# Pairs 4 to 11 of a chunked state-space scan in 64-token chunks on small TensorE tiles, ahead of a gated feed-forward layer

## The chip, the core and the metric

The kernel runs on one core of a Trainium2 chip. The metric is device time in microseconds of one execution; less is better. TensorE (PE in the profile) multiplies into eight PSUM banks, VectorE (DVE) and ScalarE (ACT) read them out, GpSimd (POOL) works on SBUF, and SyncE (SP) issues most of the DMAs.

## What is computed

Two steps. The first is a scan with a decaying state for 4 x 8 = 32 heads over 768 tokens each, head size 32 and state size 16; the second is a feed-forward layer on all 3072 tokens of 8 x 32 = 256 channels.

```python
for c in range(nc):                       # chunks; the result does not depend on their length
    cum = np.cumsum(la, axis=-1)          # la: log of the decay a, inside the chunk
    L = np.exp(cum[..., :, None] - cum[..., None, :]) * causal
    M = np.einsum('bhin,bhjn->bhij', Cc, Bc) * L
    y_intra = np.einsum('bhij,bhjd->bhid', M, xc)
    y_inter = np.einsum('bhin,bhnd->bhid', Cc, state) * np.exp(cum)[..., None]
    y[:, :, sl] = y_intra + y_inter
    Bx = np.einsum('bhjn,bhjd->bhjnd', Bc, xc) * np.exp(cum[:, :, -1:] - cum)[..., None, None]
    state = np.exp(np.sum(la, axis=-1))[..., None, None] * state + np.sum(Bx, axis=2)
# then, with x the scan's result per token:
out = (np.maximum(x @ w_gate, 0.0) * (x @ w_val)) @ w_out     # 256 -> 1536 -> 256
```

## The kernel before

The 3072 tokens are handled as 12 pairs of two 128-token chunks; three pairs make one of the four sequences. B and C are scaled beforehand with products of the decays (`scale`, line 293, on GpSimd for most pairs), so that the scan itself is left with plain matmuls: the state is a running sum, and only the causal mask stays. Four heads of 32 partitions each are laid side by side (q from 0 to 3), and two sets of four heads (t is 0 or 1) share a row of B and C in 16 of the 32 partitions each.

For a pair the steps are: `turn` transposes C and B on TensorE (line 310), ScalarE and VectorE copy them out as BT and CT. `G` (line 358) multiplies B and C of each head in four row positions of 32 rows, 128 columns wide, into four banks (g0 to g3). `gevac` (line 371) takes those 128x512 results out under the causal mask: two banks by ScalarE with GpSimd's affine_select behind it, two and a half by VectorE with a multiplication by a mask. `state` (line 407) adds a chunk's B times x in PSUM (`astep`, line 391, tile A_ps) and copies the sum out under a mask (`sevac`, line 401, tile Sm, VectorE). `inter` (line 428) multiplies the state by C into the pair's y bank, `Dm` (line 442) adds the masked G times x in four column positions of 32 columns, and `yevac` (line 456) copies y to yT in bf16, on ScalarE. Pairs 0 to 3 ("wide") hold two neighbouring tokens per partition and reach yT in two copies.

The feed-forward layer runs in six blocks of 512 tokens. In block b, pairs P = 2b+2 and Q = 2b+3 go through the scan while the layer works on pairs 2b and W = 2b+1, W being finished at the beginning of the block. `gvh` (line 484) computes gate and value for 256 tokens in one bank, `gv` (line 470) for 512 tokens in two; ScalarE applies the relu (tile r), VectorE multiplies (tile h). `fout` (line 499) is the output matmul of 128 tokens, twelve matmuls of 256 columns. A block is: a few `gvh` on the first 256 tokens, the end of W (`inter`, `Dm`, `yevac`), the same `gvh` on the second 256 tokens, eight `gv` (six in block 1) with `turn` and `state` between them, `inter` of P, then four `fout` with `G`, `state`, `Dm` of P and Q between them. Block 5 has no P and Q.

The order on every engine is the order in the program text: `in_order` fixes it at the end. The waits are set by the framework, from who writes and reads a tile. PSUM is laid out as five shared banks (`bank`, line 66: gate, value, o, G and others), one for transposes (tp), one for y, one for A_ps. SP issues each pair's six loads at the start of a block, two pairs ahead, and the output stores.

Of the kernel before, what the change touches and what calls it, by code (L numbers as in the profile page):

```python
# [29 lines left out]
def kernel(  # L30
# [23 lines left out]
    PPB = NC // 2  # L54
    NBLK = T // 512

    const = ctx.enter_context(tc.tile_pool(name="const", bufs=1))
# [8 lines left out]
    def bank(name="bank", shape=(128, 512), dtype=FP32):  # L66
        return mm.tile(list(shape), dtype, tag="shared", bufs=NSHARED, name=name)

    NWIDE = 4
    st = {}
# [89 lines left out]
    causal(masks[:, 1:2], 1, True)  # L162
    causal(masks[:, 0:1], 1, False)
    weights(0, 4)
    xb1 = att.tile([128, 2 * NH * D], BF16, tag="xb", name="xb")
    st[1]["x"] = [xb1[:, i * NH * D:(i + 1) * NH * D] for i in range(2)]
# [23 lines left out]
    def keep_warm(n, cols=512):  # L190
        w = mm.tile([128, 512], FP32, tag="y", name="w")
        for _ in range(n):
            nc.tensor.matmul(out=w[:, 0:cols], lhsT=warm[:, 0:128], rhs=warm[:, 0:cols],
                             start=True, stop=True)
# [47 lines left out]
    def new_bs(p):  # L242
        st[p]["bs"] = att.tile([128, 4, 128], BF16, tag="bs", name="bs")
        bs = st[p]["bs"]
        if p < NWIDE:
            st[p]["tin"] = [[bs[:, 2 * j + r] for r in range(2)] for j in range(2)]
        else:
            st[p]["tin"] = [[bs[:, 2 * i + j] for i in range(2)] for j in range(2)]
            st[p]["B"] = st[p]["tin"][0]
# [32 lines left out]
    def to_x(p, eng, f=None):  # L282
        xb = att.tile([128, 2 * NH * D], BF16, tag="xb", name="xb")
        xr = st[p]["xr"].rearrange("s i h d -> s (i h) d")
# [67 lines left out]
    def backevac(p, eng):  # L352
        s = st[p]
        bx = att.tile([128, 2, 128], BF16, tag="bx", name="bx")
        copy(eng, bx, s.pop("bt"))
# [35 lines left out]
    def astep(p, i):  # L391
# [3 lines left out]
        if not A_ps:  # L395
            A_ps.append(mm.tile([128, 2, 128], FP32, tag="Aps", name="A_ps"))
        nc.tensor.matmul(  # L397
# [13 lines left out]
    def y_bank(s, apart=False):  # L411
        if "y" not in s:
            if apart:
                y0 = mm.tile([128, 2, 128], FP32, tag="y", name="y")
                s["y"] = [y0, bank("y1", (128, 2, 128))]
            else:
                y = mm.tile([128, 2, 2, 128], FP32, tag="y", name="y")
                s["y"] = [y[:, 0], y[:, 1]]
                s["ya"] = y
# [36 lines left out]
    def yevac(p, *engs):  # L456
        s = st.pop(p)
        dst = yT[:, :, p * 256:(p + 1) * 256]
# [3 lines left out]
        for t in range(2):  # L462
            copy(engs[t % len(engs)],
                 dst[:, t].rearrange("q (i m r) -> q i r m", i=2, r=2),
                 s["y"][t].rearrange("q i (r m) -> q i r m", r=2))


# [58 lines left out]
    new_bs(0)  # L526
    d0 = mm.tile([128, 2, 8], FP32, tag="Aps", name="d0")
    dec_wide(d0, 0, True)
# [9 lines left out]
    bevac(0, nc.vector)  # L538
    d1 = mm.tile([128, 2, 8], FP32, tag="Aps", name="d1")
    dec_wide(d1, 1, True)  # L540
# [30 lines left out]
    bevac(1, nc.scalar)  # L571
    cevac(1, nc.vector)

    def late_decay():
# [46 lines left out]
    for b in range(NBLK):  # L621
        P, Q, W = 2 * b + 2, 2 * b + 3, 2 * b + 1
        more = P < NPAIR
        for n in (P + 2, P + 3):
            if b and n < NPAIR:
                load(n, nc.sync)

        def at(name, *fs):
            return more and f == fs[min(b, len(fs) - 1)]

        nh = 6 if b < 2 else 4
        for f in range(nh):
            if b == 0 and f < 4:
                continue
            gvh(b, f, 0)
            if b and f == (4 if b == 1 else 1):
                if b == 1:
                    state(W, 1)
                inter(W, 0)
                inter(W, 1)  # L640
                Dm(W)
                yevac(W, nc.scalar)
        for f in range(nh):
            gvh(b, f, 1)
            if b == 1 and f in (0, 3):
                scale(P if f == 0 else Q, nc.gpsimd)
        for f in range(nh, NF):
            gv(b, f)
            if b == 0 and f == 6:
                scale(P, nc.gpsimd)  # L650
                for n in (3, 4, 5):
                    held(n)
            if at("scale", 11, 99, 4):
                for n in (Q,) if b == 0 else (P, Q):
                    scale(n, nc.gpsimd)
            if at("turn P", 8, 6, 5):
                turn(P)
                tevac(P, nc.scalar, nc.vector)
            if b == 0 and f == 9:
                back(P)  # L660
                backevac(P, nc.vector)
            if at("state P0", 10, 8, 7):
                state(P, 0)
            if at("state P1", 11, 10, 9):
                state(P, 1)
            if at("turn Q", 99, 9, 8):
                turn(Q)
                tevac(Q, nc.scalar, nc.vector)
        if b == 0:
            decay()  # L670
        if more:
            inter(P, 0)
            inter(P, 1)
        fout(b, 0)
        foevac(b, 0)
        if more:
            G(P)
# [6 lines left out]
        if b == 0:  # L684
            back(Q)
            backevac(Q, nc.vector)
        if more and b > 0:
            state(Q, 0)
        if b == 0:
            for n in range(NB):  # L690
                nc.vector.reciprocal(fac[:, n, :, 0], fac[:, n, :, 1])
        fout(b, 2)
        foevac(b, 2)
        if more:
            Dm(P)
            yevac(P, nc.scalar)
            G(Q)
            gevac(Q)
            state(Q, 1 if b else 0)
        fout(b, 3)  # L700
# [33 lines left out]
```

## Time and profile before

| | us |
|---|---|
| median of three runs | 132.06 (131.21 to 132.6) |
| the profiled execution | 131.31, its span 129.5 |
| TensorE clock granted in it | 0.997 |
| block 1 in the chain, 35.41 to 54.31 | 18.90 |
| block 2, 54.31 to 72.82 | 18.51 |
| block 3, 72.82 to 91.34 | 18.52 |
| block 4, 91.34 to 109.74 | 18.40 |
| block 5, 109.74 to 126.14, no P and Q | 16.40 |

The groups of instructions that the change touches, from the page (line, engine, operation, out<-in, shapes, count, then busy us and mean ns of one, then idle time of the engine before them and what ended it):

```profile
L383 DVE TENSOR_TENSOR gs<-g,masks 128x512 bf16<-128x512 f32 x24 | 15.5, 686 | 12.8 <-PE g L364 6.4
L252 ACT CAST yT<-y 128x512 bf16<-128x512 f32 (+1 forms) x15 | 7.4, 522 | 10.5 <-PE y L449 8.2
L377 ACT CAST gs<-g 128x512 bf16<-128x512 f32 x12 | 7.1, 589 | 9.3 <-PE g L364 9.3
L405 DVE TENSOR_TENSOR Sm<-A_ps,smask 128x256 bf16<-128x256 f32 x20 | 8.3, 414 | 0.9 <-PE A_ps L397 0.9
L252 POOL CAST xb<-xr 128x512 bf16<-128x512 f32 x11 | 6.7, 613 | 2.3 <-DMA xr<-in_x_dram 1.6
```

Shown by form, the ScalarE cast to yT takes 449 ns at 128x256 and 585 at 128x512, VectorE's 446 at 128x256, the RECIPROCAL of 128x16 from PSUM (line 532) 252, and GpSimd's scaling multiplication of 128x256 (line 278) 621. Times in the chain of waits run from the end of one piece of work to the end of the next, so a piece's start there can be up to 0.2 us behind its start in the timeline. The idle column matters only for the engine that sets the end.

### The profile page before, as it was taken

The numbers are of one execution on the slowest core, as the hardware profiler recorded it, in microseconds if no ns is written. First come the engines' busy times: TensorE is split into PE (matmuls) and PEld (weight loads), VectorE is DVE, ScalarE is ACT, GpSimd is POOL, SyncE is SP. The second block draws the span as 40 slices with busy tenths as digits, with TensorE's granted clock in tenths as the row PEclk, the third lists the DMA queues.
The fourth block names the chain that finished last, engine by engine and source line by source line (L and its number), as shares of the span: only waits on it lengthen the run. The fifth ranks groups of instructions, "written<-read, shape, count | busy, mean of one in ns | idle before, by whom it ended". The sixth has DMA issues, their size and how long they took to land.

```text
span 129.5 us, 3159 instructions
## 1 busy us (share of the span) xinstructions
PE 121.3 (94%) x1144; PEld 82.2 (63%) x1151; DVE 93.4 (72%) x222; ACT 77.8 (60%) x171; POOL 42.4 (33%) x79
## 2 busy tenths in 40 slices
PE   6977889999999999999999999999999999999990
PEld 2534566468777467784567875477865577854770
DVE  4679958966987896578965878965799965587410
ACT  4063658735588754688644797745887645876410
POOL 7998591035292003390003760011930032000000
PEclk9999999999999999999999999999999999999998
DMA  3999999996999498269951198562200002200021
GB/s 65 148 178 170 177 149 178 191 143 67 118 127 202 47 126 113 86 116 113 96 86 48 41 142 119 53 95 81 83 3 0 0 5 81 81 0 0 5 103 59
DMA packets 71151, 11.97 MB, mean 92 GB/s; under 512 B 64864, under 2 KB 71072, under 8 KB 71136
## 3 DMA queue, kind: packets, MB, share of 16 engines
q1 hardware_dynamic: 63408, 8.49, 42.2%
q0 software_dynamic: 5360, 2.75, 16.5%
q10 hardware_dynamic: 2368, 0.52, 2.3%
q8 instruction: 9, 0.15, 0.5%
q14 instruction: 6, 0.05, 0.1%
HBM read 11.11 MB, written 3.15 MB: 110 GB/s over the span
## 4 chain that ended last, share of the span: by engine, by line
PE 84%; DMA 5%; DVE 5%; POOL 2%; issue 1%; SPq 1%; ACT 0%; DVEq 0%
PE o L504 25%; PE gv L492 18%; PE val L478 15%; PE gate L475 13%; DMA xr<-in_x_dram 5%; PE y L449 3%; PE g L364 3%; PE tp L310 2%; PE A_ps L397 2%; PE y L438 2%; DVE h L482 1%; DVE gs L383 1%; POOL gs L158 1%; DVE CT L332 1%; PE dall L233 1%
## 5 line engine op out<-in xcount | busy, mean ns | idle before, releaser
L504 PE MATMUL o<-wo,h 128*128 128x256 bf16 x288 | 34.7, 273 | 0.0
L482 DVE TENSOR_TENSOR h<-r,val 128x512 bf16<-128x512 bf16 x44 | 30.2, 686 | 5.1 <-ACT r L481 3.0
L481 ACT ACTIVATE r<-gate 128x512 bf16<-128x512 f32 x44 | 26.3, 597 | 9.9 <-PE gate L475 9.1
L158 POOL TENSOR_SCALAR_AFFINE_SELECT gs<-gs 128x512 bf16<-128x512 bf16 (+1 forms) x24 | 12.2, 529 | 57.0 <-ACT gs L377 57.0
L504 PEld LDWEIGHTS <-h 128*128 128x128 bf16 x288 | 27.4, 98 | 4.5 <-issue 1.3
L496 DVE TENSOR_TENSOR h<-r,gv 128x256 bf16<-128x256 bf16 x56 | 23.3, 421 | 6.6 <-ACT r L495 6.0
L478 PE MATMUL val<-yT,wv 128*128 128x512 bf16 x88 | 26.2, 379 | 0.3
L475 PE MATMUL gate<-yT,wg 128*128 128x512 bf16 x82 | 24.9, 379 | 0.0
L383 DVE TENSOR_TENSOR gs<-g,masks 128x512 bf16<-128x512 f32 x24 | 15.5, 686 | 12.8 <-PE g L364 6.4
L495 ACT ACTIVATE r<-gv 128x256 bf16<-128x256 f32 x56 | 21.5, 385 | 2.7 <-PE gv L492 0.6
L492 PE MATMUL gv<-yT,wg 128*128 128x256 bf16 x112 | 21.6, 273 | 0.1
L492 PE MATMUL gv<-yT,wv 128*128 128x256 bf16 x112 | 21.4, 272 | 0.0
L478 PEld LDWEIGHTS <-wv 128*128 128x128 bf16 x88 | 8.6, 98 | 10.4
L252 ACT CAST yT<-y 128x512 bf16<-128x512 f32 (+1 forms) x15 | 7.4, 522 | 10.5 <-PE y L449 8.2
L377 ACT CAST gs<-g 128x512 bf16<-128x512 f32 x12 | 7.1, 589 | 9.3 <-PE g L364 9.3
L492 PEld LDWEIGHTS <-wv 128*128 128x128 bf16 x112 | 10.9, 98 | 1.5 <-issue 0.2
L475 PEld LDWEIGHTS <-wg 128*128 128x128 bf16 x88 | 8.2, 98 | 5.8
L492 PEld LDWEIGHTS <-wg 128*128 128x128 bf16 x112 | 10.5, 98 | 2.0 <-issue 0.4
L278 POOL TENSOR_TENSOR bs<-bcr,fac 128x256 bf16<-128x256 f32 x16 | 9.6, 621 | 0.1
L405 DVE TENSOR_TENSOR Sm<-A_ps,smask 128x256 bf16<-128x256 f32 x20 | 8.3, 414 | 0.9 <-PE A_ps L397 0.9
L520 ACT COPY ob<-o 128x512 f32<-128x512 f32 x10 | 5.9, 585 | 4.6 <-PE o L504 4.6
L252 POOL CAST xb<-xr 128x512 bf16<-128x512 f32 x11 | 6.7, 613 | 2.3 <-DMA xr<-in_x_dram 1.6
(76 smaller groups left out, 102.9 us busy)
## 6 DMA issues: line engine op xcount, KB each, us to landing
xr<-in_x_dram SPq DMA_DIRECT2D x21, 128.0 KB, 3.5
out_dram<-ob SPq DMA_DIRECT2D x10, 256.0 KB, 2.2
bcr<-in_C_dram SPq DMA_DIRECT2D x16, 64.0 KB, 3.3
bcr<-in_B_dram SPq DMA_DIRECT2D x16, 64.0 KB, 3.1
wg<-in_moe_w_gate_dram POOLq DMA_DIRECT2D x3, 256.0 KB, 4.6
wv<-in_moe_w_val_dram POOLq DMA_DIRECT2D x3, 256.0 KB, 5.1
wo<-in_moe_w_out_dram POOLq DMA_DIRECT2D x1, 768.0 KB, 9.3
bcr<-in_C_dram SPq DMA_DIRECT2D x3, 128.0 KB, 3.6
```

Source lines behind the costliest of these rows:

```text
L158: nc.gpsimd.affine_select(out=dst, in_=dst, pattern=pattern, compare_op=ALU.is_ge, fill=0.0, base=0, channel_multiplier=-1)
L252: (eng.copy if eng is nc.scalar else eng.tensor_copy)(out=out, in_=in_)
L278: eng.tensor_tensor(out=dst[:, :, t], in0=src[:, :, t], in1=f[:, :, 4 * t:4 * t + 4].to_broadcast([128, n, 4, N]), op=ALU.mult)
L383: nc.vector.tensor_tensor(out=d[:, q], in0=g[q], in1=m, op=ALU.mult)
L475: nc.tensor.matmul(out=g, lhsT=wg[:, k, fs], rhs=yT[:, k, tk], start=(k == 0), stop=(k == 1))
L478: nc.tensor.matmul(out=v, lhsT=wv[:, k, fs], rhs=yT[:, k, tk], start=(k == 0), stop=(k == 1))
L481: nc.scalar.activation(r, g, AF.Relu)
L482: nc.vector.tensor_tensor(out=fst[b][:, f], in0=r, in1=v, op=ALU.mult)
L492: nc.tensor.matmul(out=gv_[:, j], lhsT=w[:, k, fs], rhs=yT[:, k, tk], start=(k == 0), stop=(k == 1), skip_group_check=True)
L495: nc.scalar.activation(r, gv_[:, 0], AF.Relu)
L496: nc.vector.tensor_tensor(out=fst[b][:, f, u * 256:(u + 1) * 256], in0=r, in1=gv_[:, 1], op=ALU.mult)
L504: nc.tensor.matmul(out=o[:, ts % 2], lhsT=fst[b][:, f, ts * 128:(ts + 1) * 128], rhs=wo[:, f], start=(f == 0), stop=(f == NF - 1), skip_gr ...
```

## The change

Pairs 4 to 11 go through the scan in chunks of 64 tokens, four per pair. Pairs 0 to 3 and the feed-forward layer are computed as before.

- `G64` computes only the blocks of 64 by 64 tokens that are needed, in 32 matmuls of 128 columns (two sets t of 64) on sixteen 32x32 tiles, again into four banks of half the width. `gevac64` takes them out as 128x256: q 0 and 1 by ScalarE and a GpSimd multiplication by a 64-column mask, q 2 and 3 by VectorE.
- `A64` computes each chunk's own B times x, without accumulation, in 16 matmuls of 64 columns on 64x32 tiles. `sums` lets VectorE add them up in fp32 (tile F, 64 columns, one operation per chunk), and GpSimd copies the result to bf16 (tile Sc). `carry` does this for pair 3, whose parts `A64(4, True)` computes.
- `inter64` has 32 matmuls of 64 columns on the four diagonal 32x32 tiles (24 in a sequence's first pair), `D64` 32 of 64 columns on 64x32 tiles.
- y and the states of a pair lie in one tile of two banks (`ya`), the bank chosen by the chunk's parity r. ScalarE copies y of r = 0 to yT, VectorE that of r = 1. The y bank, A_ps, the warm-up and the first decay tiles of pairs 0 to 3 lie in the first such tile (`ya0`).
- Steps move: `inter` of P goes behind the third `fout`, state work of P from the `gv` steps to the end of W, `scale` of the next P into the tenth feed-forward step of a block. xb and bs get six buffers in place of three, bx four.

In the program as built, TensorE's instruction list has 3556 rows in place of 2232.

```diff
+    def new_ya():
+        return mm.tile([128, 2, 512], FP32, tag="ya", name="ya")
+    ya0 = new_ya()
...
-        w = mm.tile([128, 512], FP32, tag="y", name="w")
+        w = ya0[:, 0]
...
-            A_ps.append(mm.tile([128, 2, 128], FP32, tag="Aps", name="A_ps"))
+            A_ps.append(ya0[:, 1, 256:512].rearrange("p (t m) -> p t m", t=2))
...
-                y = mm.tile([128, 2, 2, 128], FP32, tag="y", name="y")
+                y = ya0[:, 0].rearrange("p (t i m) -> p t i m", t=2, i=2)
...
+    ya = []
+    def rows(r):
+        return slice(64 * r, 64 * r + 64)
+    def quad(q):
+        return slice(32 * q, 32 * q + 32)
+    def y64(r, t=None, i=None):
+        y = ya[0][:, r, 0:256].rearrange("p (t i m) -> p t i m", t=2, i=2)
+        return y if t is None else y[:, t, i]
+    def A64(p, new=False):
+        if new:
+            ya[:] = [new_ya()]
+        todo = [(i, p, i) for i in range(2)]
+        if new:
+            todo += [(2, p - 1, i) for i in range(2)]
+        for k, e, i in todo:
+            xi = st[e]["x"][i].rearrange("s (t q d) -> s q t d", t=2, q=4)
+            for q in range(4):
+                for r in range(2):
+                    nc.tensor.matmul(
+                        out=ya[0][quad(q), r, 256 + 64 * k:320 + 64 * k].rearrange(
+                            "p (t d) -> p t d", t=2),
+                        lhsT=st[e]["B"][i][rows(r), quad(q)], rhs=xi[rows(r), q],
+                        start=new, stop=True, tile_position=(64 * r, 32 * q),
+                        skip_group_check=True)
+            new = False
+        st[p]["As"] = [ya[0][:, r, 256:448].rearrange("p (k e) -> p k e", e=64)
+                       for r in range(2)]
+    F, Sb = {}, {}
+    def new_F(p):
+        F[p] = att.tile([128, 4, 64], FP32, tag="F", name="F", bufs=2)
+        Sb[p] = att.tile([128, 4, 64], BF16, tag="Sc", name="Sc", bufs=4)
+    def carry(p):
+        new_F(p - 1)
+        f, a = F[p - 1][:, 3], st[p]["As"]
+        nc.vector.tensor_copy(f, a[0][:, 2])
+        nc.vector.tensor_tensor(out=f, in0=f, in1=a[1][:, 2], op=ALU.add)
+        nc.gpsimd.tensor_copy(Sb[p - 1][:, 3], f)
+    def sums(p):
+        new_F(p)
+        a, f = st[p]["As"], F[p]
+        k0 = p % PPB
+        n = 3 if k0 == PPB - 1 else 4
+        for c in range(n):
+            ac = a[c % 2][:, c // 2]
+            if c == 0 and k0 == 0:
+                nc.vector.tensor_copy(f[:, 0], ac)
+            else:
+                nc.vector.tensor_tensor(
+                    out=f[:, c], in0=f[:, c - 1] if c else F[p - 1][:, 3], in1=ac,
+                    op=ALU.add)
+        nc.gpsimd.tensor_copy(Sb[p][:, 0:n], f[:, 0:n])
+    def inter64(p):
+        s = st[p]
+        first = p % PPB == 0
+        ya[:] = [new_ya()]
+        s["open64"] = [False, False]
+        for c in range(int(first), 4):
+            i, r = c // 2, c % 2
+            for t in range(2):
+                new, s["open64"][r] = not s["open64"][r], True
+                for q in range(4):
+                    nc.tensor.matmul(
+                        out=y64(r, t, i)[quad(q)],
+                        lhsT=(Sb[p][quad(q), c - 1] if c else Sb[p - 1][quad(q), 3])[
+                            :, 32 * t:32 * t + 32],
+                        rhs=s["CT"][quad(q), t, i, rows(r)],
+                        start=new, stop=False, tile_position=(32 * q, 32 * q),
+                        skip_group_check=True)
+    def G64(p):
+        s = st[p]
+        s["gp"] = g = [bank("g%d" % q, (128, 2, 2, 64)) for q in range(4)]
+        for i in range(2):
+            for h in range(4):
+                for q in range(4):
+                    nc.tensor.matmul(
+                        out=g[q][quad(h), i],
+                        lhsT=s["BT"][quad(q), i, quad(h)],
+                        rhs=s["CT"][quad(q), :, i, rows(h // 2)],
+                        start=(i == 0), stop=True, tile_position=(32 * q, 32 * h),
+                        skip_group_check=True)
+        s["gs"] = att.tile([128, 4, 4, 64], BF16, tag="gs", name="gs", bufs=2)
+    def gevac64(p, qs=(0, 2, 1, 3)):
+        s = st[p]
+        d = s["gs"]
+        m = mask64.rearrange("p (o m) -> p o m", o=1).to_broadcast([128, 4, 64])
+        for q in qs:
+            g = s["gp"][q].rearrange("j i t m -> j (i t) m")
+            if q < 2:
+                nc.scalar.copy(out=d[:, q], in_=g)
+                nc.gpsimd.tensor_tensor(out=d[:, q], in0=d[:, q], in1=m, op=ALU.mult)
+            else:
+                nc.vector.tensor_tensor(out=d[:, q], in0=g, in1=m, op=ALU.mult)
+    def D64(p):
+        s = st[p]
+        for t in range(2):
+            for i in range(2):
+                for q in range(4):
+                    for r in range(2):
+                        nc.tensor.matmul(
+                            out=y64(r, t, i)[quad(q)],
+                            lhsT=s["x"][i][rows(r), (4 * t + q) * D:(4 * t + q + 1) * D],
+                            rhs=s["gs"][rows(r), q, 2 * i + t],
+                            start=False, stop=True, tile_position=(64 * r, 32 * q),
+                            skip_group_check=True)
+        s["y64"] = [y64(r) for r in range(2)]
+    def yevac64(p):
+        dst = yT[:, :, p * 256:(p + 1) * 256].rearrange("q t (i r m) -> q r t i m", i=2, r=2)
+        for r, eng in ((0, nc.scalar), (1, nc.vector)):
+            copy(eng, dst[:, r], st[p]["y64"][r])
...
+    for r in range(2):
+        nc.vector.tensor_copy(mask64[64 * r:64 * r + 64], masks[64 * r:64 * r + 64, 0, 64 * r:64 * r + 64])
...
+        new = b and more
         for n in (P + 2, P + 3):
             if b and n < NPAIR:
                 load(n, nc.sync)
-
-        def at(name, *fs):
-            return more and f == fs[min(b, len(fs) - 1)]
         nh = 6 if b < 2 else 4
         for f in range(nh):
             if b == 0 and f < 4:
                 continue
             gvh(b, f, 0)
-            if b and f == (4 if b == 1 else 1):
-                if b == 1:
-                    state(W, 1)
+            if b == 1 and f == 4:
                 inter(W, 0)
                 inter(W, 1)
                 Dm(W)
                 yevac(W, nc.scalar)
+            if b > 1 and f == 1:
+                inter64(W)
+                D64(W)
+                if more:
+                    A64(P)
+                yevac64(W)
         for f in range(nh):
             gvh(b, f, 1)
             if b == 1 and f in (0, 3):
                 scale(P if f == 0 else Q, nc.gpsimd)
         for f in range(nh, NF):
             gv(b, f)
-            if b == 0 and f == 6:
-                scale(P, nc.gpsimd)
-                for n in (3, 4, 5):
-                    held(n)
-            if at("scale", 11, 99, 4):
-                for n in (Q,) if b == 0 else (P, Q):
-                    scale(n, nc.gpsimd)
-            if at("turn P", 8, 6, 5):
-                turn(P)
-                tevac(P, nc.scalar, nc.vector)
-            if b == 0 and f == 9:
-                back(P)
-                backevac(P, nc.vector)
-            if at("state P0", 10, 8, 7):
-                state(P, 0)
-            if at("state P1", 11, 10, 9):
-                state(P, 1)
-            if at("turn Q", 99, 9, 8):
-                turn(Q)
-                tevac(Q, nc.scalar, nc.vector)
+            if b == 0:
+                if f == 6:
+                    scale(P, nc.gpsimd)
+                    for n in (3, 4, 5):
+                        held(n)
+                if f == 8:
+                    turn(P)
+                    tevac(P, nc.scalar, nc.vector)
+                if f == 9:
+                    back(P)
+                    backevac(P, nc.vector)
+                if f == 10:
+                    state(P, 0)
+                if f == 11:
+                    scale(Q, nc.gpsimd)
+                    state(P, 1)
+            elif more:
+                if f == (6 if b == 1 else 5):
+                    turn(P)
+                    tevac(P, nc.scalar, nc.vector)
+                if f == 5 and b > 1:
+                    scale(Q, nc.gpsimd)
+                if f == 8 and b == 1:
+                    A64(P, True)
+                    carry(P)
+                    sums(P)
+                if f == 9:
+                    turn(Q)
+                    tevac(Q, nc.scalar, nc.vector)
+                    if Q + 1 < NPAIR:
+                        scale(Q + 1, nc.gpsimd)
         if b == 0:
             decay()
-        if more:
             inter(P, 0)
             inter(P, 1)
         fout(b, 0)
         foevac(b, 0)
-        if more:
+        if new:
+            if b > 1:
+                sums(P)
+            G64(P)
+            gevac64(P)
+        elif more:
             G(P)
             gevac(P)
         if b == 0:
         if b == 0:
             back(Q)
             backevac(Q, nc.vector)
-        if more and b > 0:
-            state(Q, 0)
-        if b == 0:
             for n in range(NB):
                 nc.vector.reciprocal(fac[:, n, :, 0], fac[:, n, :, 1])
         fout(b, 2)
         foevac(b, 2)
-        if more:
+        if new:
+            inter64(P)
+            G64(Q)
+            gevac64(Q, (0, 2))
+            D64(P)
+            A64(Q)
+            yevac64(P)
+            gevac64(Q, (1,))
+            sums(Q)
+            gevac64(Q, (3,))
+        elif more:
             Dm(P)
             yevac(P, nc.scalar)
             G(Q)
             gevac(Q)
-            state(Q, 1 if b else 0)
+            state(Q, 0)
         fout(b, 3)
         foevac(b, 3)
```

## What the change does to the time: the prediction

> **What bounds the kernel now.** I read the page's busy shares first, then the chain of waits, then one block of that chain, and at last the timelines of VectorE and ScalarE where the change touches them. On the page, the first two columns after an engine's name are its busy time and share of the span:
>
> ```profile
> PE 121.3 (94%) x1144; PEld 82.2 (63%) x1151; DVE 93.4 (72%) x222; ACT 77.8 (60%) x171; POOL 42.4 (33%) x79
> ...
> PEclk9999999999999999999999999999999999999998
> ```
>
> TensorE is busy nearly throughout, at an undisturbed clock. Busy alone does not make it the bound, since matmuls overlap. The chain of waits (start, length in us, what) does. It shows the end of block 2 and the first part of block 3:
>
> ```profile
> 66.05 0.11 PE y L438 x2
> 66.16 1.31 PE o L504 x12
> 67.47 0.33 PE g L364 x8
> 67.80 1.42 PE o L504 x12
> 69.21 0.11 PE A_ps L397
> 69.32 1.31 PE o L504 x12
> 70.63 0.34 PE y L449 x16
> 70.97 0.33 PE g L364 x8
> 71.30 0.22 PE A_ps L397
> 71.51 1.31 PE o L504 x12
> 72.82 0.87 PE gv L492 x8
> 73.70 0.22 PE y L438 x4
> 73.92 0.34 PE y L449 x16
> 74.26 2.73 PE gv L492 x24
> ```
>
> No other engine stands between these pieces: from 35.4 to 126 us the time is the sum of what TensorE streams. A removed column gives its time back, and every new wait on the way costs in full, because there is no idle time to put it in.
>
> The unit prices come from the same rows. Twelve 256-column matmuls take 1.31 us, so 0.109 each; the four 128-column ones of L438 take 0.22, so 0.055 each: the time is that of the columns. G (8 matmuls, four row positions side by side) is two turns of 256 columns, 0.22, and takes 0.33; D (16 matmuls, four column positions) is four turns of 128 columns, 0.22, and takes 0.34. The output piece behind G takes 1.42 in place of 1.31. So each change of tile shape costs about 0.11.
>
> **Part 1, the matmuls.** A block has two pairs, and the previous block's last pair is finished in it. Before, per block: inter 8 x 0.055 = 0.44, G 0.44, D 0.44, states 4 x 0.109 = 0.44, and seven changes of shape, 0.77: 2.5 us (2.8 with 0.44 of transposes less a few skipped matmuls; the block's 18.51 us less 15.7 of feed-forward work leaves 2.84).
>
> After: G64 has sixteen positions at once, so 32 matmuls are two turns of 128 columns, 0.11 a pair. D64 (eight positions) is four turns of 64 columns, the state matmuls two, inter64 (four diagonal positions) eight: fourteen a pair. Shape changes become eight, 0.88: finishing the older pair goes from full tiles to 32x32, 64x32 and back, three changes where inter and D had two. What is not in the trace is a turn of 64 columns. By columns it is 0.028; if a tile cannot turn round faster than in D, 0.055. I take 0.033, near the columns, because D's turns show no more than their columns although every matmul there brings its own weights. So 28 x 0.033 + 0.22 + 0.88 = 2.0 per block, 0.5 less than before; over blocks 1 to 4, **2.1 us saved** (bounds: 2.7 saved, 0.4 lost). Block 1's extra: pair 3's states are computed again and the sixteen-turn piece stands between feed-forward matmuls with two shape changes (0.35), against three state matmuls removed (0.33): nothing.
>
> **Part 2, who waits in the blocks.** Evacuations shrink: VectorE gives up 2 x 0.686 + 2 x 0.414 per pair for 256-wide pieces and the sums, ScalarE 0.59 + 0.39 + 0.59 for three pieces of about 0.4. That earns nothing, as neither is on the chain; what counts is order. In the program as built, VectorE's half of the y copy waits for ScalarE's half, and both stand before the sums. The sums are 64 columns wide: between 0.21 (the line through 0.414 at 256 and 0.686 at 512 columns) and 0.25 (the 16-column RECIPROCAL, 0.252); I take 0.24, each waiting for the last.
>
> From the end of a block's last D64: ScalarE 0.05 later, 0.45; VectorE 0.41; four sums 0.96; GpSimd's copy 0.36 (half of L252's 0.613 and a start) with two handovers of 0.05: 2.3 us until the next inter64 may go on. TensorE arrives after 1.31 + 0.87 and two shape changes, less the 0.2 by which a matmul starts ahead of its end: 2.2. Late by about 0.15 after four sums, not at all after three: 0.3 in all. Queued behind the waiting weight load are the rest of inter64, D64 and all later feed-forward work.
>
> Then the pair's y: ScalarE 0.45, VectorE 0.41 after it, handovers 0.15, 1.0 us, where now one 0.59 copy does. TensorE's cover is 0.87 of gv matmuls and a shape change, less 0.2: 0.8. Late by 0.2 in each of blocks 2 to 5: 0.8. **Together 1.1 us lost** (0 to 2).
>
> **Part 3, waits that come with the shared tile.** All y banks, the state bank and the warm-up now lie in one two-bank tile, and the built program orders readers and writers of the whole tile. ScalarE and VectorE in the trace of before, near pair 1 and pair 2 (start, length):
>
> ```profile
> 17.70 0.76 ACT L252 CAST yT<-y 128x256 bf16<-128x256 f32 x2 [1.51 <-PE y L449]
> ...
> 17.90 0.42 DVE L405 TENSOR_TENSOR Sm<-A_ps,smask 128x256 bf16<-128x256 f32 x1 [0.93 <-PE A_ps L397]
> ...
> 33.61 0.76 ACT L252 CAST yT<-y 128x256 bf16<-128x256 f32 x2 [1.19 <-PE y L449]
> ```
>
> Pair 1's yT must now wait for the Sm that ends at 18.32, and then ends at 19.1; TensorE reads it at about 18.6: 0.45 lost (0.2 to 0.6). Pair 3's state matmul, at 33.9 in the chain, must wait until pair 2's yT is out at 34.37: 0.5 (0.2 to 0.6). In block 1, six dependent operations (the carried state and four sums, 1.45 us) enter VectorE's queue between two h products and two Sm (0.67 net, since they overlap) leave it. The last h now ends at 48.46, the twelfth output matmul needs it at about 48.8; 0.78 later, it is late by 0.55 (0.2 to 0.9). The two mask copies lie in VectorE's part of the start-up chain: 0.1 (0 to 0.25). **1.6 us lost.** The next first pair's scale moves from the next block to the tenth feed-forward step of this one: 2 x 0.62 and 0.61 on GpSimd, now ahead of the Sc copy and the masks. SP's queue is as before; in block 2 it issues that pair's six loads from 55.4 to 59.8, they land 3.5 later, and scale is done by 65.2, before the sums that Sc needs are made (after the last h, 66.5). The cover goes if a load is over 1.5 us later; then inter64 of the same block, at 71, still has 4 us. So nothing.
>
> Sum against the profiled execution, which took 131.31 us (span 129.5): 131.31 - 2.1 + 1.1 + 1.6 = 131.9. The three runs' median, 132.06, lies 0.75 above that execution, so the forecast is **132.7**.
>
> **Rivals.**
>
> *The cover holds.* The waits of part 2 fit into the output matmuls, those of part 3 go at their low ends (0.4, and 0.55 in block 1, 0.1 for the masks), and turns cost their columns: 131.31 - 2.7 + 1.05 = 129.7, by the median 130.4. For it: D's turns, and VectorE idle for 1.55 us ahead of a G evacuation in block 1. Against it: VectorE's share of 72%, the serial halves.
>
> *Issue decides.* 224 matmuls per block take the place of 60, and each has its own weight load. The longest such run in the trace is D followed by G, 24 matmuls; a run of 112 has none to compare with. If each needs a turn of its own, as D's stretch gives when divided by its count (0.34/16 = 0.021 us), a block pays 224 x 0.021 = 4.7 in place of 2.5: 8.8 more over four blocks, 141 by the median with the losses partly covered. It decides from about 0.011 each: there part 1's gain is gone and the losses stay, 134.8. For it: nothing shows a long run sustained. Against it: four tiles of one turn overlap in D and G. The Trainium skill, "TensorE: Matmul & The Clock Gate", section "Wait — 56ns, not 53.3ns?", says that starts of successive matmuls never come closer than about 25 ns however small they are; an estimate by it alone would be 5.6 us per block, some 12 us more in all. Taken over all tiles, D's row of 0.021 including its shape change speaks against that rule.
>
> *One bank for four row positions.* G spreads its row positions over four banks; inter64's four write one. If they go one behind another, its 64 matmuls per block take 64 x 0.028 = 1.8 in place of 0.53: 5.1 more, 137.8. The trace has no such form. The Trainium skill, "TensorEngine Tiling (Array Packing)", section "Restrictions and Gotchas", says that different row tiles cannot access the same PSUM bank simultaneously; no run here shows whether that holds for disjoint partitions.
>
> **How the numbers follow.** Forecast 0.38, its own range 131.4 to 134.0; cover holds 0.28 (129.6 to 131.3); issue 0.27 (134.8 to 141); one bank 0.07. A measurement of this kernel tells about 1% from no change: 130.7 to 133.4. Faster: 0.22 of the second case. Same: 0.28 of the first and 0.06 of the second. Slower: 0.10 of the first, and the last two: 0.44. The range leaves out the fastest 0.07 and the upper half of the issue case: 130.0 to 138.0.
>
> **What would show it.** Right: in the chain, G64 pieces of about 0.22 with their shape change, inter64 of 0.25 to 0.3, D64 of about 0.13 plus a change; short VectorE or GpSimd pieces ahead of the finished pair's inter64, and VectorE's yT ahead of the first gv matmul on the new tokens. Issue: inter64, G64 and D64 near 0.7 each. One bank: inter64 alone near 0.9. Wrong altogether if the blocks' length stays at 18.5 with no waits, or if the loss lies in start-up.

## The result, and the profile after

The changed kernel takes 136.11 us (median of 4 runs, 135.68 to 136.65), the kernel before 132.33 in the four runs beside it. It is 1.032 times as long, 95% interval 1.023 to 1.041; one slow run of the kernel before, 133.78 us, is left out of this ratio. The profiled execution took 135.71 us (span 134.0), that of before 131.31 (span 129.5).

First the page of the changed kernel, the lines that answer to those of before:

```profile
PE 124.6 (93%) x1813; PEld 84.2 (63%) x1813; DVE 91.3 (68%) x241; ACT 74.9 (56%) x171; POOL 48.2 (36%) x88
...
PEclk9965899999999999999999999999999999999999
```

TensorE has 669 more recorded matmuls and nearly as high a share as before. The clock row differs: in this execution the granted clock was at half from about 8 to 14 us. That need not be the change's doing: a second trace of the kernel before, below, has the same.

Second the chain of waits from the end of block 2 (start, length in us, what), the same stretch as before:

```profile
69.17 1.31 PE o L639 x12
70.48 0.26 PE g L563 x32
70.74 2.73 PE o L639 x24
73.46 0.22 PE ya L549 x14
73.68 0.03 PE g L563 x3
73.71 0.04 PE ya L549 x7
73.75 0.28 PE g L563 x26
74.03 0.29 PE ya L589 x32
74.33 0.18 PE ya L499 x16
74.51 1.42 PE o L639 x12
75.93 0.87 PE gv L627 x8
76.80 0.34 PE ya L549 x26
77.14 0.20 issue
77.34 0.23 PE ya L549 x6
77.57 0.24 PE ya L589 x32
```

L549 is inter64, L563 G64, L589 D64 and L499 A64 (a few records are missing, so counts fall short). The chain is still nearly TensorE's own: the change did not put another engine into the middle of the blocks. But the same 32 matmuls of G64 take 0.26 with their shape change at 70.48, and 0.28 at 73.75 where no shape changes; and at 77.14 stands a piece called "issue", a step in the middle of inter64 for which no releaser is shown.

Third, where the chain leaves TensorE, at pairs 1 and 3 and in block 1 (three stretches of the chain):

```profile
18.95 0.23 PE ya L404
...
19.20 0.44 DVE Sm L412
...
19.66 0.45 ACT yT L259
...
35.01 0.37 PE ya L456 x16
...
35.40 0.76 ACT yT L259 x2
...
36.20 0.27 PE ya L404
...
50.12 1.28 DVE h L617 x2
...
51.45 0.28 PE o L639
```

These are the three waits of part 3: pair 1's yT behind Sm, pair 3's state matmul behind pair 2's yT, the output matmul behind h products that the carried state and the sums have pushed back.

The starts of the first gv matmul of each block, read from the start times of the matmuls, give the lengths of the stages (us; block 5 is counted to the start of the last output matmul):

```
                block 1 starts   block 1   2       3       4       5
before               35.25       18.90   18.51   18.51   18.40   16.20
before, 2nd trace    36.24       18.90   18.51   18.51   18.40   16.20
changed              37.61       19.47   18.68   19.17   18.84   16.47
changed, 2nd trace   37.89       19.48   18.68   18.82   18.83   16.47
```

The same start times, with the feed-forward matmuls, the transposes and the wait for the y copy taken off, give what the attention matmuls of a block cost, shape changes included: block 2 2.42 before and 2.44 after. The 0.5 that part 1 was to save is not there.

### The profile page after: what moved, and what is told of

Same layout as the page of the kernel before. It is cut to its first block, busy times and chain, and to the rows that moved or that the text cites. A ratio compares the mean times of both kernels' runs of the same rounds, so it can differ in the third digit from the quotient of the medians.

```text
span 134.0 us, 4501 instructions
## 1 busy us (share of the span) xinstructions
PE 124.6 (93%) x1813; PEld 84.2 (63%) x1813; DVE 91.3 (68%) x241; ACT 74.9 (56%) x171; POOL 48.2 (36%) x88
## 4 chain that ended last, share of the span: by engine, by line
PE 84%; DVE 8%; ACT 2%; DMA 2%; issue 1%; DVEq 0%
PE o L639 23%; PE gv L627 18%; PE gate L610 14%; PE val L613 13%; PE ya L549 2%; DMA a_sb<-in_a_dram 2%; DVE h L617 2%; PE tp L317 2%; PE ya L589 2%; PE g L563 2%; ACT yT L259 2%; PE ya L200 1%; PE ya L499 1%; PE ya L456 1%; PE ya L404 1%
## 5 line engine op out<-in xcount | busy, mean ns | idle before, releaser
L610 PE MATMUL gate<-yT,wg 128*128 128x512 bf16 x88 | 26.2, 379 | 0.0
L627 PE MATMUL gv<-yT,wg 128*128 128x256 bf16 x112 | 22.2, 277 | 0.8 <-DVE h L631 0.5
L627 PE MATMUL gv<-yT,wv 128*128 128x256 bf16 x112 | 21.9, 278 | 0.0
L579 POOL TENSOR_TENSOR gs<-gs,mask 128x256 bf16<-128x256 bf16 x16 | 10.5, 669 | 9.6 <-ACT gs L578 9.3
L581 DVE TENSOR_TENSOR gs<-g,mask 128x256 bf16<-128x256 f32 x16 | 6.4, 420 | 11.0 <-PE g L563 10.9
L578 ACT CAST gs<-g 128x256 bf16<-128x256 f32 x16 | 5.6, 375 | 12.4 <-PE g L563 12.4
L537 POOL CAST Sc<-F 128x256 bf16<-128x256 f32 (+1 forms) x8 | 3.0, 378 | 20.8 <-DVE F L534 20.5
L259 ACT CAST yT<-ya 128x256 bf16<-128x256 f32 x15 | 5.7, 407 | 8.6 <-PE ya L404 2.4
```

The costliest lines, as they stand in the source:

```text
L259: (eng.copy if eng is nc.scalar else eng.tensor_copy)(out=out, in_=in_)
L579: nc.gpsimd.tensor_tensor(out=d[:, q], in0=d[:, q], in1=m, op=ALU.mult)
L581: nc.vector.tensor_tensor(out=d[:, q], in0=g, in1=m, op=ALU.mult)
L610: nc.tensor.matmul(out=g, lhsT=wg[:, k, fs], rhs=yT[:, k, tk], start=(k == 0), stop=(k == 1))
L627: nc.tensor.matmul(out=gv_[:, j], lhsT=w[:, k, fs], rhs=yT[:, k, tk], start=(k == 0), stop=(k == 1), skip_group_check=True)
```

## The experiments

The theories were two at first. A: the many small matmuls are limited by the rate at which TensorE is given instructions. B: the loss is in the waits that come with the two-bank tile. (For the two edits of G64 the expectations use B for another rival, that the columns streamed through the array bound it.) Theory F, on the fetching of instructions, and theory Q, on a store ahead of TensorE, came up on the way.

**Two one-bank tiles.** y and states of chunk parity 0 and 1 each get a tile of their own (the other uses of the tile change alike):

```diff
-        return mm.tile([128, 2, 512], FP32, tag="ya", name="ya")
+        return [mm.tile([128, 512], FP32, tag="ya%d" % r, name="ya%d" % r) for r in range(2)]
...
-        y = ya[0][:, r, 0:256].rearrange("p (t i m) -> p t i m", t=2, i=2)
+        y = ya[0][r][:, 0:256].rearrange("p (t i m) -> p t i m", t=2, i=2)
```

> The changed kernel with the two-bank tile cut into two tiles of one bank each; nothing else. Built, the two halves of the y copy wait only for TensorE, and pair 3's state matmul and pair 1's yT wait for no other bank's reader. Theory A (the loss in the blocks is TensorE's issue of small matmuls, and the shared tile costs only the two waits at the start): block 1 begins 1.0 to 1.1 us earlier than the changed kernel's 37.6, blocks 2 to 5 keep 18.7, 19.2, 18.8 and 16.5 within 0.2 each, 134.6 to 135.2 us in all. Theory B (the shared tile is most of the loss): block 1 begins at 35.3 as in the kernel before, blocks 2 to 5 lose another 0.2 each, 132.5 to 133.3.

133.74 us (133.17 to 133.92), 1.016 times before [1.011, 1.021]: 2.4 us below the changed kernel, between the two theories. In its trace block 1 begins at 36.42, 1.19 earlier, with the same half clock; the waits at pair 1 and pair 3 are gone, and so is the series of the two y copies, which cost 0.15, 0.14, 0.13 and 0.22 in blocks 2 to 5. Its block 1 is 0.52 longer, most of it one step without a wait (0.47, in the table below). The timeline of VectorE in the changed kernel shows this series; its half waits for ScalarE's, not for TensorE:

```profile
78.53 0.42 DVE L259 CAST yT<-ya 128x256 bf16<-128x256 f32 x1 [0.86 <-ACT yT L259]
```

**G64 twice.**

```diff
-        for i in range(2):
+        for i in (0, 1, 0, 1):
             for h in range(4):
```

> The changed kernel with every G64 issued twice over (64 matmuls in place of 32 per pair, same result). Theory A (past those that wait ready in its queue, TensorE issues one small matmul with its weight load per 8.3 ns): the 32 more cost 0.27 us per pair, 2.1 us in all over eight pairs, and their starts lie 8.3 ns apart throughout the second half. Theory B (turns of columns on the array bound it): two more turns of 128 columns, 0.11 per pair, 0.9 in all. If each matmul needs a turn of 21 ns as in my second rival: 0.67 per pair, 5.4 in all.

140.88 us (140.26 to 141.32), 1.070 times before [1.065, 1.076]: 4.8 over the changed kernel, more than twice what A expected. By the start times, the second G64 of a block costs exactly 32 x 8.3 ns = 0.27 more, as A said. The first one does not: its 32 matmuls start 3.3 ns apart, then nothing starts for 136 ns, then the 32 added ones follow 8.3 ns apart, 0.40 more. And there are long steps without a wait, the longest in the chain of block 4, in an output piece:

```profile
116.72 0.65 PE o L639 x5
117.37 1.23 issue
118.61 0.60 PE o L639 x4
```

**G64 in tiles of 32x64**, 16 matmuls with 64 weight columns in place of 32.

```diff
-            for h in range(4):
+            for h in range(2):
...
-                        out=g[q][quad(h), i],
-                        lhsT=s["BT"][quad(q), i, quad(h)],
+                        out=g[q][rows(h), i],
+                        lhsT=s["BT"][quad(q), i, rows(h)],
```

> The changed kernel with G64 in 16 matmuls per pair instead of 32: 64 weight columns (one whole chunk of 64 tokens) on 32x64 tiles, eight positions, the same 256 columns of turns per pair. Theory A (issue at 8.3 ns per matmul): the piece of G64, D64 and states behind inter64 gets 0.13 shorter per block, the G64 ahead of the second output matmuls at most 0.05, so 0.6 to 0.7 us in all. Theory B (turns of columns): no change. An extra change of tile shape between inter64 (32x32) and G64 (32x64), 0.1 per block, would take 0.4 of it back.

136.02 us (135.08 to 136.49), 1.035 times before [1.029, 1.041]: no gain that can be told. The burst of inter64, G64, D64, A64 shrinks from 1.21 to 1.16 and not by more, since the new tile shape brings one more change.

**Block 1's sums later**, the carried state and the sums behind the first output piece.

```diff
                 if f == 8 and b == 1:
                     A64(P, True)
-                    carry(P)
-                    sums(P)
...
         if new:
-            if b > 1:
-                sums(P)
+            if b == 1:
+                carry(P)
+            sums(P)
```

> The changed kernel with carry and sums of block 1 moved from the ninth feed-forward step to behind the first output matmuls, as blocks 2 to 4 have them. If the six VectorE operations between two h products make the twelfth output matmul late, the gap of 0.49 us at 51.5 goes and block 1 is 0.4 to 0.5 shorter (19.0); the whole is 135.6 to 135.8. If the gap has another cause (ScalarE's relu of that step), block 1 stays at 19.4 to 19.5.

136.17 us (135.47 to 137.22), 1.036 times before [1.029, 1.043]. The stall of 0.49 in block 1 is gone, and the block takes 18.99 in place of 19.47. The total is no lower: in this execution block 1 began at 38.78, 1.17 later than in the changed kernel, on a clock that fell to half a second time. So single profiles differ by about 1 us in the start-up alone, and the edit is read from its block.

**Steps without a wait.** Each such step longer than 0.3 us, in all traces until then, stood at nearly the same place when TensorE's recorded instructions are counted modulo 256 (186 to 194), and ended 2.35 to 2.91 us after a 16 KB packet of the instruction queue began. The kernel before moves 9 such packets, the changed one 14 (packets, MB, share):

```profile
q8 instruction: 9, 0.15, 0.5%
...
q8 instruction: 14, 0.23, 0.7%
```

From this came theory F, and this edit, which adds 64 instructions ahead of everything:

```diff
     keep_warm(6, 128)
+    for k in range(32):
+        q = h = k % 4
+        nc.tensor.matmul(out=ya0[32 * h:32 * h + 32, 0, 0:16], lhsT=warm[32 * q:32 * q + 32, 0:32],
+                         rhs=warm[32 * q:32 * q + 32, 0:16], start=True, stop=True,
+                         tile_position=(32 * q, 32 * h), skip_group_check=True)
```

> The changed kernel with 32 extra small matmuls (16 columns, 32x32 tiles) where TensorE waits at 5.6 us: 64 more instructions ahead of everything, nothing else. In the traces so far, the steps of TensorE without any wait (0.38 us in block 3 of the changed kernel; 0.47 in the split one; 0.49, 0.33 and 1.51 in the one with G64 twice) all stand at the same place in TensorE's count of instructions modulo 256 (recorded counts 1986, 1213, 1470, 2237, 3770: remainders 194, 189, 190, 189, 186), and each ends 2.35 to 2.9 us after a 16 KB packet of the instruction queue began. Theory F (instruction fetch): TensorE cannot cross two such boundaries in less than about 3.2 us; the padding moves the boundaries 64 instructions ahead, where the changed kernel's own times leave 3.3 us or more between them; so the 0.38 in block 3 goes, and no step without a wait over 0.25 us stands off the new boundaries; the time is 0 to 0.8 lower than the changed kernel's. Rival S (block 3's inter64 waits for its states in a way that the trace does not show): the step stays where it is, about 0.4 long, and the time is the same or 0.3 higher.

136.45 us (135.93 to 137.05), 1.038 times before [1.031, 1.045]. The step in block 3 is gone (18.78 in place of 19.17) and no step over 0.25 is left, as F expects, but the time is not lower: its block 1 begins 0.55 later. It settles less than was hoped, for the changed kernel run once more, unedited, had no such step either:

> The changed kernel once more, for a second trace: its unprofiled runs took 136.5 to 136.65 at a granted clock of 1.0 over the run and 135.7 at 0.975. Theory F: what is longer in a run at full clock is steps without a wait at the 256-instruction boundaries (more than the one of 0.38 us), while block 1 begins earlier than 37.6. Rival: the start-up alone varies, and blocks 2 to 5 are as before, 18.68, 19.17, 18.84 and 16.47 within 0.1.

135.64 us (one run). Its mean clock is given as 1.0, but the clock record of this trace begins only at 12.8 us, and ahead of that the matmuls ran at half clock. The three warm-up matmuls of 512 columns, first in the changed kernel's first trace, at a recorded half clock, then in this one:

```profile
8.60 1.49 PE L200 MATMUL ya<-warm 128*128 128x512 bf16 x3
...
9.41 1.49 PE L200 MATMUL ya<-warm 128*128 128x512 bf16 x3
```

In both they start 0.427 apart; in the blocks, matmuls of this size start 0.216 apart. So a mean clock of 1.0 does not show a full clock in the start-up, and the expectation, which took it so, fails in its premise. Block 1 begins at 37.89 (the first transpose stood 0.7 later than in the first trace), blocks 2, 4 and 5 repeat within 0.01, and block 3 takes 18.82. So the step in block 3 comes and goes; by theory F, a fetch is in time or not.

> The kernel before once more, for a second trace: four of its seven runs had a clock of 0.997 or 1.0 (131.05 to 131.8 us) and three 0.974 to 0.987 (131.9 to 132.1). If this profile shows a clock below 0.99, the half clock lies between 7 and 15 us and block 1 begins 0.5 to 1.2 us later than 35.25: so much of the changed kernel's late start is the clock and not the change. If the clock is full, block 1 begins at 35.1 to 35.5. Blocks 1 to 5 as before within 0.1, with no step without a wait over 0.25 us.

132.22 us (one run), and this execution had the half clock, from 7.5 to 14.3 us. Its page:

```profile
PEclk9965899999999999999999999999999999999999
```

Block 1 begins 0.99 later than in the first trace of before, at 36.24, and the blocks repeat to 0.01. Of the 2.36 us by which the changed kernel's first block began later than in that trace, 1.37 is left between two traces with the same half clock; this is put to the change, with the start-up's own spread in it. All ten traces of the changed kernel and its variants have the half clock for 6 us or more between 5 and 16 us, and of the two of the kernel before one has it. Whether the change makes it more frequent is not shown.

**Both, shifted**: G64 twice and the padding, edits as above.

> The kernel with G64 issued twice, and the 32 small matmuls of the padding at 5.6 us ahead of everything: its 256-instruction boundaries move 64 instructions ahead. In its earlier trace, the times between successive boundaries (from 43 us on: 9.8, 3.7, 3.9, 12.0, 3.8, 3.8, 12.0, 3.9, 3.5, 9.8, 6.0, 3.4) are never below 3.39 us, while at 64 instructions ahead of them the same trace has 2.74 (from 76.2 us), 1.14 (from 95.8) and 2.06 (from 114.2). Theory F (instruction fetch, one chunk of 256 in about 3.3 us or more): these three can't stay: all become 3.2 or more, by steps without a wait of 0.5, 2.1 and 1.2 us or their like in the bursts of blocks 3, 4 and 5 counted from 0 at the new boundaries, and the three old steps (0.49, 0.33, 1.51) go; time 140.5 to 143.5. Rival S (steps that belong to certain instructions): the old three stay within 0.2 us of their size at their instructions, and nothing new appears: 141 to 142.

140.05 us (one run). The three old steps are gone, and three new ones stand at other instructions, where the boundaries now lie: 0.46 in an inter64, 0.86 in a gv piece and 0.37 in an A64. The chain at the second, where the kernel before has plain feed-forward work:

```profile
78.30 0.22 PE gv L627 x2
78.52 0.59 issue
79.11 0.50 PE gv L627 x3
```

All eight steps, with the recorded instructions ahead of each and the time from the start of the last instruction packet to the end of the step. A step is the time from one start to the next; the two longest lie between matmuls that otherwise start 0.11 apart:

```
kernel            instructions   modulo 256   step us   packet to end us
changed               1986          194         0.38         2.81
two tiles             1213          189         0.47         2.41
G64 twice             1470          190         0.49         2.91
G64 twice             2237          189         0.33         2.35
G64 twice             3770          186         1.51         2.84
twice, shifted        1470          190         0.46         2.98
twice, shifted        2237          189         0.86         2.32
twice, shifted        3004          188         0.37         2.60
```

The place goes with the count and not with the instruction: rival S falls. F's spacing falls too. It wanted 3.2 us or more between any two boundaries, and this trace has 1.50 and 2.06, so more than one piece can lie ready. What remains shown is that TensorE at times stands still at a fixed place in a count of 256 instructions, until 2.3 to 3.0 us after a packet began.

**Refill.** Three long matmuls in the middle of the burst:

```diff
             inter64(P)
+            fout(b, 3, 0, 3)
             G64(Q)
...
-        fout(b, 3)
+        fout(b, 3, 3 if new else 0)
```

> The changed kernel with the first 3 of the 12 matmuls of the last output piece between inter64 and G64 of the second pair, in blocks 1 to 4: 0.33 us of long matmuls in the middle of the burst. In the traces, the 32 matmuls of G64 behind an output piece start 3.3 ns apart (0.117 us in all) and those behind inter64 8.3 ns apart (0.250). Theory Q (a store of some 64 instructions ahead of TensorE, which inter64's 32 matmuls and 32 weight loads use up; what comes then arrives at 4.15 ns an instruction): the long matmuls let the store fill, G64 takes 0.11 to 0.14 again and A64, last, stays at 8.3 ns each. Rival R (8.3 ns is the price of G64's form behind inter64, of its weights or its banks): G64 stays at 0.25. Two more shape changes cost 0.2 a block and the y copy has 0.33 less cover, so the time is 0.5 to 1.5 above the changed kernel's in either case.

136.82 us (one run). TensorE's timeline (start, length with the end of the last one, in us) in block 4, first of the changed kernel:

```profile
111.33 0.41 PE L549 MATMUL ya<-CT,Sc 32*32 32x64 bf16 x32
111.57 0.47 PE L563 MATMUL g<-CT,BT 32*32 32x128 bf16 x32
111.97 0.36 PE L589 MATMUL ya<-gs,xb 64*32 64x64 bf16 x32
112.20 0.32 PE L499 MATMUL ya<-xb,bs 64*32 64x64 bf16 x16
```

Then of this run:

```profile
112.22 0.41 PE L549 MATMUL ya<-CT,Sc 32*32 32x64 bf16 x32
112.56 0.50 PE L639 MATMUL o<-wo,h 128*128 128x256 bf16 x3
112.99 0.33 PE L563 MATMUL g<-CT,BT 32*32 32x128 bf16 x32
113.25 0.50 PE L589 MATMUL ya<-gs,xb 64*32 64x64 bf16 x32
113.56 0.32 PE L499 MATMUL ya<-xb,bs 64*32 64x64 bf16 x16
```

G64 behind the three long matmuls has 0.116 between its first and last start, against 0.250 in the changed kernel's burst, as Q expects; R falls. Now D64, which comes next, is the slow one, 8.3 ns a matmul and 0.301 against 0.166. So the slow pace belongs to the place behind 64 instructions, and not to the form of the matmuls.

**All three edits**, two tiles, later sums and G64 in 32x64.

> Three edits of the runs before together: y and states in two one-bank tiles, block 1's sums behind its first output piece, G64 in 16 matmuls of 64 weight columns in place of 32. If the costs stand beside each other: the split run's 133.74, less 0.5 for the sums, less 0.05 x 6 for G64, and fewer instructions to fetch: 132.9 (132.4 to 133.4), ratio to before 1.004 to 1.012. If the cost of issue was hidden behind a wait that the edits only move: 133.5 or more.

132.76 us (median of 10 runs, 131.96 to 135.0), 1.008 times before [1.005, 1.012], as expected if the costs stand side by side. The chain over the same stretch:

```profile
68.51 0.25 PE g L563 x16
68.75 2.73 PE o L639 x24
71.48 0.28 PE ya L549 x24
71.76 0.25 PE g L563 x16
72.01 0.32 PE ya L589 x32
72.33 0.16 PE ya L499 x16
```

Its blocks take 18.91, 18.48, 18.54, 18.49 and 16.25, and block 1 begins at 36.35: against the second trace of before, at the same half clock, nothing differs by more than 0.11. That is the cleanest reading of part 1: with the three waits of the shared tile and of block 1 taken out, matmuls in 64-token chunks, G64 in its 16-matmul form, cost what those in 128-token chunks did. The interval of the ratio still leaves 0.4 to 1.2% of loss. No version tried was faster than the kernel before.

## Why the prediction went as it did

The number 136.1 lies in the stated range, but above the forecast's own, 131.4 to 134.0: it is the range's width, made for the rivals, that holds it. It lies in the *Issue decides* case by luck in part, since that case gives 134.8 at the price that was measured, and what goes beyond it was in no part of the prediction. Against the second trace of before, at the same half clock, the profiled execution is 3.49 longer: 1.37 in the start-up, 0.57 in block 1, 0.17, 0.66 and 0.44 in blocks 2 to 4, 0.27 in block 5 and after. By the steps of the prediction:

**The bound** was read rightly: the chain stays on TensorE, and the added waits show as gaps between TensorE's own starts. Of the loss, 1.37 of 3.49 lies in the start-up, which the text had named as a sign of being wrong altogether; 1.06 of it are the two waits that part 3 had placed there.

**Part 1 is the step that failed.** It said that 28 turns at 0.033 and eight shape changes make 2.0 per block, "because D's turns show no more than their columns although every matmul there brings its own weights". The turns are right for the first 32 matmuls behind long ones: G64 0.117 from its first start to its last, inter64 29 ns a turn. The shape changes were about 0.093, below the 0.11 taken, 0.14 less for eight. But D is 16 matmuls long, and a burst of 112 outruns what is ready. In block 2, from a piece's first start to that of the next and with shape changes taken off, the G64 between output pieces takes 0.17 in place of 0.11, inter64 with the G64 behind it 0.48 in place of 0.31, each D64 0.23 in place of 0.13 and each A64 0.16 in place of 0.07. That is 0.6 more, and with the cheaper shape changes the 0.5 by which this block's 2.44 exceeds the prediction's 1.96 (its first pair starts a sequence and has two turns fewer). Over blocks 1 to 4 the 2.1 us saved turned into a loss of about 0.4: with the waits and steps taken off, they came out 0.1, 0.0, 0.2 and 0.1 above before. (The bound of 2.7 saved comes to 2.6 by the text's own figures; nothing hangs on it.)

**Part 2** had the right waits and too high a price for one: 0.64 for the y copies against 0.8, and about 0.15 in all for inter64's wait for its states (0.11 in block 4, 0.03 in block 3) against 0.3.

**Part 3** came out nearly as priced: pair 1's yT 0.48 (0.45), pair 3's state matmul 0.58 (0.5), block 1 0.49 (0.55). The mask copies, priced at 0.1, do not show: from the first gv matmul to pair 1's last state matmul the changed kernel takes 0.04 longer. Two tiles took 1.2 to 1.3 out of the start-up, a little more than the two waits in it.

**Not in the prediction** were the fetch step of 0.38 in block 3, a smaller one of 0.10 in block 4's A64, and 0.28 by which the first gv matmul already starts later (12.51 against 12.23), 0.19 of it ahead of the first transpose. Added up, the forecast of 132.7 with 2.5 more for part 1, 0.3 less for part 2, 0.5 for the steps and 0.3 for the start-up is 135.7, the time of the profiled execution.

**The rivals.** *Issue decides* named the cause. Its price of 0.021 a matmul was far too high; measured with shape changes it is 2.44/216 = 0.0113 in block 2, right at the 0.011 from which the text said that part 1's gain is gone. The rule of the Trainium skill, "TensorE: Matmul & The Clock Gate", section "Wait — 56ns, not 53.3ns?", of 25 ns between starts however small the matmul, does not hold over tiles side by side: starts were 3.3 ns apart with instructions ready and 8.3 without. *One bank for four row positions* falls: inter64's four tiles start 3.3 ns apart and take 29 ns a turn, the time of 64 columns, while writing one bank. The Trainium skill's "TensorEngine Tiling (Array Packing)", section "Restrictions and Gotchas", says that different row tiles cannot access one bank at the same time; for four tiles that write different partitions of it, this trace shows otherwise. *The cover holds* falls with part 3.

## What to carry to other kernels

Cutting columns by cutting matmuls into small tiles pays only as long as instructions arrive: price a burst by both its columns and its count, here 4.15 ns an instruction (8.3 for a matmul with its weights) beyond the first 64, and compare a burst with the longest run of small matmuls that the trace holds before trusting its turns. When tiles that had banks of their own are put into one, follow every pair of reader and writer in the program as built; these waits could be priced to within 0.1 us from the trace alone. And before the start-up of two profiles is compared, look at the spacing of the matmuls in both, and not at the clock row alone: one row here read full where the spacing was that of half clock.

## What the runs showed of the hardware

- Some 64 instructions are ready ahead of TensorE when long matmuls run. Where 32 matmuls and 32 weight loads have used them up at 3.3 ns a matmul, nothing started for 136 ns (G64 twice), and from there on one came every 8.3 ns. That this is a store with a refill delay is inferred from these starts; the runs show the starts.
- At times TensorE stands still at a fixed place in a count of 256 instructions, for up to 1.4 us, with no semaphore in the trace; the same kernel showed it in one run and not in the next. That it waits for an instruction packet is inferred from the place and from the 2.3 to 3.0 us between the packet's start and the step's end. When it comes is not settled; nor is why two runs of the changed kernel with a mean clock of 1.0 took 136.5 and 136.65 us, of which there is no trace.
- TensorE ran at half clock for some 6 us or more of the start-up in every trace of the changed kernel and its variants, and in one of the two of the kernel before, whose block 1 began 0.99 later in it than in the other. In two traces the clock record starts too late to show it (12.8 and 13.1 us), and the spacing of the warm-up matmuls does. What decides it was not tried.
